# A spectral layer's second exchange: two of eight back steps copied inside SBUF, the others read back from DRAM one back step at a time

## The chip, the cores and the metric

The kernel runs on one core of a Trainium2 chip. The metric is the device time of one execution in microseconds; less is better. In the traces PE is TensorE, DVE is VectorE, ACT is ScalarE, POOL is GpSimd and SP is SyncE, which here issues nearly all DMAs. Times inside an execution count from the start of the profiled span.

## The reference

The input x has 2048 rows (S) of 512 columns (D), in bfloat16. Two layers alternate, twice each:

```python
def _A_ref(x, w_r, w_i):
    X = jnp.fft.rfft2(x.astype(jnp.float32), axes=(-2, -1))
    X = X * (w_r + 1j * w_i)
    return jnp.fft.irfft2(X, s=(S, D), axes=(-2, -1)).astype(jnp.bfloat16)

x = x + _A_ref(_layernorm(x), A_w_r, A_w_i)      # spectral layer
x = x + _B_ref(_layernorm(x), wq, wk, wv, wo)    # attention: 32 heads of 16, one shared key and value head
x = x + _A_ref(_layernorm(x), A_w_r, A_w_i)
x = x + _B_ref(_layernorm(x), wq, wk, wv, wo)
```

The change is in the spectral layer. It filters x in the two-dimensional frequency domain and transforms back.

## The kernel before

Each spectral layer is written as matrix products with tables of sines and cosines, in bfloat16, with sums in PSUM. The 2048 rows are split as 128 by 16, so a transform over the rows takes two products with an exchange of partitions between them. Columns are in two halves (h = 0, 1) of 128 frequencies, real and imaginary part side by side, 256 values in all.

Forward, `forward` (L275) transforms the columns, `first` (L285 by way of `rotate`, L214 to L216) does the first product over the rows, and the result goes to DRAM (D1, L290) and comes back with other partitions (A2, `cross1`, L293). This is the first exchange; it isn't changed.

Then the layer works in eight back steps, j = 0 to 7. Steps 0 to 3 belong to half 0 and steps 4 to 7 to half 1; each covers four blocks b of the 16. `filtered(j)` (f) does the forward product of these blocks, evicts it (ACT, L339) and multiplies by the filter (DVE, L343 and L345). `back(j)` (b) multiplies with the tables H1, H2, H2N, H1N, two blocks to a PSUM bank, evicts the bank into B1 (L375 on ACT; the last bank of step 7 on DVE, L373), and writes these two blocks of B1 to the DRAM buffer D2 (L376, on SP's queue). The tables H are made on POOL by `blocks` (L266), as the product of a small table HC and a mask.

The second exchange is `cross2` (L379): one call reads a quarter of the rows t of D2 into B2, for all 128 partitions. Each half takes four such reads of 256 KB. A read needs all four back steps of its half, since every row of B2 holds something of each. The reads of half 0 are the step x0 in a list of steps written out by hand (`STEPS`, L50):

```python
STEPS = "f0 f1 f2 b0 f3 b1 b2 j f4 b3 x0 f5 f6 b4 f7 b5 j7 b6 b7"
```

After the list, `along(q, 0)` (L401) multiplies B2 of half 0 by the table CS, two rows t at a time, eight times, and ACT and DVE in turn evict into AT (L404, L406). Then the four reads of half 1 are issued, two from SP and two from ACT, then the loads of wq and wo (L1225, L1226, in the first layer). TensorE starts the first four `last(t, 0)` (L414 to L416), which need half 0 only, and goes on with `along(q, 1)` (L401 again) and the rest of `last`. ACT evicts the result into x_sb (L435), and layer norm statistics (L157) and the first projections of attention (L472) follow.

The order on each engine's queue is the order of the program text (`manual_schedule`), and an instruction that waits holds up those behind it in its queue. DMAs issued by one engine complete on semaphores that are used in turn. Attention is planned ahead, when the program is built, and its order doesn't depend on times on the chip. The spectral layer occurs twice, at 0 to 92 us and at about 704 to 784 us of the span.

Of the kernel before, what the change touches and what calls it, by code (L numbers as in the profile page):

```python
# [10 lines left out]
ALU = mybir.AluOpType  # L11
P = 128
BF = mybir.dt.bfloat16
# [4 lines left out]
S, D, H, DH = 2048, 512, 32, 16  # L18
# [28 lines left out]
LASTW = 6  # L47
NEGATE = 7
DIRECT = (0, 2, 4, 6)
STEPS = "f0 f1 f2 b0 f3 b1 b2 j f4 b3 x0 f5 f6 b4 f7 b5 j7 b6 b7"  # L50
NORMED, NORMG = (1,), ((3,), (3,), (3,))
OUTK, LATE_AT = 2, 4
TWICE = ((7,), 8)
# [23 lines left out]
def host_tables():  # L77
    import ml_dtypes
    bf = lambda a: np.ascontiguousarray(np.asarray(a, dtype=np.float32).astype(ml_dtypes.bfloat16))
    tabs = {}  # L80
    p = np.arange(P, dtype=np.float64)
    m = np.arange(P, dtype=np.float64)
    t16 = np.arange(16, dtype=np.float64)

    row = (128 * np.arange(4)[None, :, None] + np.arange(P)[:, None, None]).astype(np.float64)
    ff = (np.arange(256)[None, None, :] + 1).astype(np.float64)

    half = 2 * np.pi * np.arange(256) / 512.0
    cos, sin = np.cos(half), np.sin(half)
    cos[128], sin[0] = 0.0, 0.0  # L90
    cos[129:], sin[129:] = -cos[1:128][::-1], sin[1:128][::-1]
    turn = (row * ff).astype(np.int64) % 512
    c, s = np.concatenate([cos, -cos])[turn], -np.concatenate([sin, -sin])[turn]
    tabs["PH"] = bf(np.concatenate([c[..., :128], s[..., :128], c[..., 128:], s[..., 128:]], axis=2))

    ang = 2 * np.pi * (16 * p[:, None, None] + t16[None, :, None]) * m[None, None, :] / 2048.0
    tabs["C1"], tabs["S1"] = bf(np.cos(ang)), bf(np.sin(ang))

    ti, ai = np.divmod(np.arange(P), 8)
    same = (ai[:, None] == ai[None, :]).astype(np.float64)  # L100
    ang = 2 * np.pi * ti[:, None] * ti[None, :] / 16.0
    tabs["G"] = bf(np.stack([same * np.cos(ang), same * np.sin(ang), -same * np.sin(ang)], axis=1))

    b16 = np.arange(16, dtype=np.float64)
    mm = 16 * ai[:, None, None] + b16[None, :, None]
    ang = 2 * np.pi * (ti[:, None, None] * t16[None, None, :] / 16.0 + t16[None, None, :] * mm / 2048.0)
    tabs["HC"] = bf(np.stack([np.cos(ang), np.sin(ang), -np.sin(ang), -np.cos(ang)], axis=1))
    tabs["mask8"] = bf(ai[:, None] == np.arange(8)[None, :])

    ang = 2 * np.pi * m[:, None] * p[None, :] / 128.0  # L110
    tabs["CS"] = bf(np.stack([np.concatenate([np.cos(ang), np.sin(ang)], axis=1),
                              np.concatenate([-np.sin(ang), np.cos(ang)], axis=1)], axis=1))

    frow = (128 * np.arange(2)[None, :, None] + np.arange(P)[:, None, None] + 1).astype(np.float64)
    dd = np.arange(512)[None, None, :].astype(np.float64)
    ang = 2 * np.pi * frow * dd / 512.0
    cf = np.where(frow == 256, 1.0, 2.0) / (S * D)
    tabs["PSC"] = bf(cf * np.cos(ang))
    tabs["PSS"] = bf(-cf * np.sin(ang))
    tabs["ident"] = bf(np.eye(P, dtype=np.float32))  # L120
    tabs["hmask"] = (np.arange(P)[:, None] // DH % 2 == np.arange(2)[None, :]).astype(np.float32)
    return tabs


class Tables:


    def __init__(self, nc):
        self.nc, self.host, self.dram = nc, host_tables(), {}
# [82 lines left out]
def rotate(nc, ps, c, s, sn, re_im, first, begin=True, end=True):  # L212

    nc.tensor.matmul(ps, lhsT=c, rhs=re_im, start=begin, stop=False, skip_group_check=True)  # L214
    nc.tensor.matmul(ps[:, 0:128], lhsT=s, rhs=re_im[:, 128:256], start=False, stop=False, skip_group_check=True)
    nc.tensor.matmul(ps[:, 128:256], lhsT=sn, rhs=re_im[:, 0:128], start=False, stop=end, skip_group_check=True)  # L216


def spectral_layer(nc, tc, tabs, ht, A_w_r, A_w_i, x_sb, bigp, pre, norm, att, feed, weights):
    C1, S1, S1N, PH, ident = (tabs[n] for n in ("C1", "S1", "S1N", "PH", "ident"))  # L220
    with tc.tile_pool(name="workA", bufs=2) as work, tc.tile_pool(name="tabA", bufs=1) as tabA, \
# [31 lines left out]
            weights(k)  # L253

        D1 = dram.tile([2, 16, P, 256], BF, name="D1")
        D2 = dram.tile([2, P, 16, 256], BF, name="D2")
        turned = len(feed.xT)
        xT = feed.xT[0] if turned else bigp.tile([P, NC, 16, P], BF, name="xT", tag="big")
        Pk, A1, A2 = big("Pk"), big("A1"), big("A2")
# [1 line left out]
        def blocks(q):  # L261

            b = slice(4 * q, 4 * q + 4)
            shape = [P, 4, 16, 8]
            for i, H in enumerate([H1[:, b], H2[:, b], H2N[:, b]] + ([H1N[q]] if q in H1N else [])):
                nc.gpsimd.tensor_tensor(out=H.rearrange("p b (t a) -> p b t a", a=8),  # L266
                                        in0=tabs["HC"][:, i, b].unsqueeze(3).to_broadcast(shape),
                                        in1=tabs["mask8"].unsqueeze(1).unsqueeze(1).to_broadcast(shape), op=ALU.mult)

        def forward(k, h):  # L270

# [26 lines left out]
        for k in range(9 + behind):  # L298
# [6 lines left out]
            at = k - behind  # L305
# [21 lines left out]
        Z, B1, B2 = big("Z"), big("B1"), big("B2")  # L327
        M = big("M").rearrange("p h t c -> p (h t c)").rearrange("p (i j b r f) -> p i j b r f", i=2, j=4, b=4, r=2)

        def filtered(j):  # L330

            h, b4 = j // 4, 4 * (j % 4)
            hf = slice(128 * h, 128 * h + 128)
            X = work.tile([P, 4, 2, 128], BF, name="X", tag="X", bufs=3)
            for b in range(b4, b4 + 4, 2):
                ps = bank()
                for i in range(2):
                    rotate(nc, ps[:, i, :], G[:, 0, :], G[:, 1, :], G[:, 2, :], A2[:, h, b + i, :], i == 0)
                nc.scalar.copy(out=X[:, b - b4:b - b4 + 2, :, :], in_=ps.rearrange("p j (r f) -> p j r f", r=2))  # L339
            m1, m2 = (M[:, i, j % 4] for i in range(2))  # L340
            wrb = wr_sb[:, b4:b4 + 4, hf].unsqueeze(2).to_broadcast([P, 4, 2, 128])
            wib = wi_sb[:, b4:b4 + 4, hf].unsqueeze(2).to_broadcast([P, 4, 2, 128])
            nc.vector.tensor_tensor(out=m1, in0=X, in1=wrb, op=ALU.mult)  # L343
            joined()
            nc.vector.tensor_tensor(out=m2, in0=X, in1=wib, op=ALU.mult)  # L345
            if j in DIRECT:
                unsummed[j] = (m1, m2)
            else:
                products.append((j, m1, m2))
# [3 lines left out]
        def joined():  # L353

            while products:
                j, m1, m2 = products.pop()
                Zv = Z[:, j // 4, 4 * (j % 4):4 * (j % 4) + 4, :].rearrange("p b (r f) -> p b r f", r=2)
                nc.vector.tensor_tensor(out=Zv[:, :, 0, :], in0=m1[:, :, 0, :], in1=m2[:, :, 1, :], op=ALU.subtract)
                nc.vector.tensor_tensor(out=Zv[:, :, 1, :], in0=m1[:, :, 1, :], in1=m2[:, :, 0, :], op=ALU.add)

        def back(j):
            h, b4 = j // 4, 4 * (j % 4)
            for b in range(b4, b4 + 4, 2):
                ps = bank()
                for i in range(2):
                    if j in DIRECT:
                        m1, m2 = (m[:, b + i - b4].rearrange("p r f -> p (r f)") for m in unsummed[j])
                        rotate(nc, ps[:, i, :], H1[:, b + i, :], H2N[:, b + i, :], H2[:, b + i, :], m1, i == 0, True, False)
                        rotate(nc, ps[:, i, :], H2N[:, b + i, :], H1N[j % 4][:, b + i - b4, :], H1[:, b + i, :], m2, False, False)
                    else:  # L370
                        rotate(nc, ps[:, i, :], H1[:, b + i, :], H2N[:, b + i, :], H2[:, b + i, :], Z[:, h, b + i, :], i == 0)
                if j == 7 and b > b4:
                    nc.vector.tensor_copy(out=B1[:, h, b:b + 2, :], in_=ps)  # L373
                else:
                    nc.scalar.copy(out=B1[:, h, b:b + 2, :], in_=ps)  # L375
                nc.sync.dma_start(out=D2[h, :, b:b + 2, :], in_=B1[:, h, b:b + 2, :])  # L376

        def cross2(h, g, eng):
            eng.dma_start(out=B2[:, h, 4 * g:4 * g + 4, :],  # L379
                          in_=D2[h].rearrange("(t a) b c -> t (a b) c", t=16)[4 * g:4 * g + 4].rearrange("t m c -> m t c"))  # L380

        for step in STEPS.split():
            j = int(step[1:] or 0)
            if step[0] == "f":
                filtered(j)
            elif step[0] == "b":
                back(j)
            elif step[0] == "j":
                joined()
            else:  # L390
                for g in range(4):
                    cross2(0, g, nc.sync)

        AT = big("AT").rearrange("p h t c -> p (h t c)").rearrange("p (t h c) -> p t h c", t=16, h=2)

# [21 lines left out]

        for q in range(8):
            along(q, 0, q % 2 == 0)
        for g in range(4):  # L420
            cross2(1, g, (nc.sync, nc.scalar)[g % 2])
        weights(20)
        early = 4
        for t in range(early):
# [2 lines left out]
        for q in range(9):  # L427
# [9 lines left out]
            g, odd = divmod(q - 3, 2)  # L437
# [863 lines left out]
```

## Time and profile before

| | us |
|---|---|
| median of 3 runs | 1403.78 |
| lowest and highest run | 1402.68, 1403.95 |
| profiled execution, its time | 1402.49 |
| its span | 1400.7 |
| TensorE busy | 1348.2 (96%) |
| ScalarE busy | 1331.4 (95%) |
| VectorE busy | 1305.8 (93%) |
| GpSimd busy | 849.4 (61%) |
| DMA D2<-B1 (L376), 128 KB, issue to landing | 3.0 median of 32 |
| DMA B2<-D2 (L379), 256 KB, issue to landing | 3.9 median of 12 on SP, 4.4 median of 4 on ACT |
| DMA A2<-D1 (L293), 256 KB, issue to landing | 3.3 median of 16 |

The profile names a tile without its number, so B is B1 or B2, D is D1 or D2, and A is A1 or A2. "SPq" is SP's queue: an issue of a DMA, not the transfer. In the chain of work that ended last, each line is a start, a length and what ran; a DMA there runs from its issue to its landing. In the timeline a bracket gives the idle time ahead of an instruction and what ended it. In the table by stretches, the last two columns are the mean busy share of the core's 16 DMA engines and the GB/s that they moved.

### The profile page before, as it was taken

What the parts mean: (1) busy time and instruction counts of PE and PEld (TensorE: products, weight loads), DVE (VectorE), ACT (ScalarE), POOL (GpSimd) and SP (SyncE); (2) the same over time, 40 slices, a digit from 0 to 9 for tenths busy, and PEclk for the clock granted to TensorE, in tenths of its full rate; (3) what the DMA queues carried; (4) which work ended last, traced back from release to release, by engine and by line L of the source; (5) the groups of instructions that cost most, each with busy time, mean ns of one, the idle gap of its engine ahead of it and who ended that gap; (6) DMA issues with size and microseconds to landing.
All of it is one profiled execution on the core that took longest, in us unless ns stands there. A gap on an engine that the chain in (4) does not pass through costs nothing.

```text
span 1400.7 us, 35023 instructions
## 1 busy us (share of the span) xinstructions
PE 1348.2 (96%) x14146; PEld 477.7 (34%) x14214; DVE 1305.8 (93%) x2253; ACT 1331.4 (95%) x1542; POOL 849.4 (61%) x507
## 2 busy tenths in 40 slices
PE   7899999999999999999999999999999999999998
PEld 6752232222222222222277422322223222222222
DVE  5689999999999999999966899999999999999997
ACT  6679999999999999999957899999999999999997
POOL 3325666667666667666640367666667667666664
PEclk9999999999999999999999999999999999999999
DMA  8700000000000000002064000000000000000000
GB/s 243 209 17 2 1 2 2 2 2 2 2 1 1 2 2 2 2 1 37 11 166 137 2 2 2 2 1 9 5 6 2 6 9 5 2 6 5 9 2 16
DMA packets 45395, 32.70 MB, mean 23 GB/s; under 512 B 10160, under 2 KB 43184, under 8 KB 44720
## 3 DMA queue, kind: packets, MB, share of 16 engines
q1 hardware_dynamic: 42832, 29.24, 7.4%
q8 instruction: 111, 1.82, 0.5%
q10 hardware_dynamic: 2400, 1.21, 0.3%
q14 instruction: 52, 0.43, 0.1%
HBM read 18.39 MB, written 10.49 MB: 21 GB/s over the span
## 4 chain that ended last, share of the span: by engine, by line
ACT 48%; PE 33%; issue 9%; DVE 6%; DMA 2%; POOL 1%; SPq 0%; DVEq 0%; ACTq 0%; POOLq 0%
ACT e L1099 47%; PE pv L888 13%; PE sc L933 10%; DVE ph L973 3%; PE aux L933 2%; PE ps L214 1%; PE ps L275 1%; DVE ln_stats L157 1%; PE aux L472 1%; DMA B<-D 1%; DVE ph L1005 1%; PE pv L903 1%; PE aux L701 1%; POOL tab_H L266 1%; PE ps L216 1%
## 5 line engine op out<-in xcount | busy, mean ns | idle before, releaser
L1099 ACT ACTIVATE e<-sc 128x1024 bf16<-128x1024 f32 x1328 | 1218.1, 1163 | 2.9 <-PE sc L933 2.9
L997 POOL TENSOR_TENSOR ph<-ph,step 128x1024 int32<-128x1024 int32 x404 | 763.3, 1893 | 412.3 <-DVE ph L1005 291.8
L973 DVE TENSOR_SCALAR ph<-aux 128x512 uint16<-128x512 f32 x1440 | 904.0, 679 | 20.4 <-PE aux L933 15.8
L888 PE MATMUL pv<-ph,vaug 128*32 128x512 bf16 x4320 | 548.8, 386 | 0.6 <-POOL ph L997 0.3
L933 PE MATMUL sc<-QT,Kv 32*128 32x512 bf16 x2656 | 521.9, 380 | 23.2 <-ACT e L1099 15.9
L888 PE MATMUL pv<-e,vaug 128*32 128x512 bf16 x2656 | 484.0, 384 | 0.3 <-ACT e L1099 0.3
L933 PE MATMUL aux<-QT,Kv 32*128 32x512 bf16 x1440 | 456.0, 384 | 1.0 <-DVE ph L973 0.5
L933 PEld LDWEIGHTS <-Kv 32*128 32x128 bf16 x4096 | 183.2, 91 | 525.5 <-issue 517.2
L903 PE MATMUL pv<-wo_sb,zeros 128*32 128x512 bf16 x1200 | 257.9, 383 | 0.0
L888 PEld LDWEIGHTS <-vaug 128*32 128x32 bf16 x6976 | 147.7, 94 | 293.0 <-issue 282.0
L1005 DVE TENSOR_SCALAR ph<-ph 128x2048 uint16<-128x2048 uint16 x316 | 216.6, 685 | 0.5
L163 POOL TENSOR_TENSOR ln_rstd<-ln_veps,mhalf 128x4 f32<-128x4 f32 x16 | 16.5, 1034 | 107.2 <-DVE ln_veps L162 107.1
L157 DVE BATCH_NORM_STATS2 ln_stats<-x_sb 128x6 f32<-128x512 bf16 x64 | 43.5, 679 | 23.3 <-ACT x_sb L435 17.2
L903 PEld LDWEIGHTS <-zeros 128*32 128x32 bf16 x1200 | 60.1, 94 | 1.9 <-issue 0.3
L803 DVE STREAM_TRANSPOSE oT<-pv 128x512 f32<-128x512 f32 x64 | 45.3, 707 | 9.2 <-PE pv L888 9.2
L186 ACT ACTIVATE Pk<-ps,ln_rstd 128x256 bf16<-128x256 f32 x64 | 26.7, 473 | 21.0 <-PE ps L275 16.1
L289 DVE CAST A<-ps 128x512 bf16<-128x512 f32 x28 | 19.2, 689 | 19.8 <-PE ps L216 18.7
L275 PE MATMUL ps<-tab_PH,xT 128*128 128x256 bf16 x256 | 35.6, 288 | 1.7 <-DMA tab_PH<-const_PH 0.8
L472 PE MATMUL aux<-xTa,wq_sb 128*128 128x512 bf16 x90 | 32.6, 385 | 2.8 <-issue 2.4
L825 POOL TENSOR_TENSOR on<-oT,rden 128x512 bf16<-128x512 f32 x30 | 31.7, 1058 | 2.0 <-DVE rden L829 1.8
L701 PE MATMUL aux<-wo_sb,ph 128*128 128x512 bf16 x72 | 26.1, 383 | 3.6 <-issue 2.1
L275 PEld LDWEIGHTS <-xT 128*128 128x128 bf16 x256 | 25.4, 103 | 6.0 <-issue 1.5
(117 smaller groups left out, 715.2 us busy)
## 6 DMA issues: line engine op xcount, KB each, us to landing
D<-A SPq DMA_DIRECT2D x32, 128.0 KB, 2.7
A<-D SPq DMA_DIRECT2D x16, 256.0 KB, 3.3
D<-B SPq DMA_DIRECT2D x32, 128.0 KB, 3.0
B<-D SPq DMA_DIRECT2D x12, 256.0 KB, 3.9
wr_sb<-in_A_w_r_dram SPq DMA_DIRECT2D x2, 1024.0 KB, 7.0
wi_sb<-in_A_w_i_dram SPq DMA_DIRECT2D x2, 1024.0 KB, 8.9
out_dram<-x_sb SPq DMA_DIRECT2D x15, 128.0 KB, 1.7
x_sb<-in_A_x_dram SPq DMA_DIRECT2D x3, 512.0 KB, 8.2
```

Source lines behind the costliest of these rows:

```text
L157: nc.vector.bn_stats(st, src)
L275: nc.tensor.matmul(ps[:, j, :], lhsT=xT[:, cc, 2 * k + j, :], rhs=PH[:, cc, 256 * h:256 * h + 256], start=(cc == 0), stop=(cc == NC - 1), ...
L472: self.nc.tensor.matmul(ps, lhsT=w(c), rhs=self.xTq[:, c, qc * 512:(qc + 1) * 512], start=(c == 0), stop=(c == NC - 1), skip_group_check=True)
L701: nc.tensor.matmul(ps, lhsT=OTs[qb][:, g4, kk * P:(kk + 1) * P], rhs=wo_sb[:, g4, :], start=first, stop=last, skip_group_check=True)
L803: end = clock.now(clock.FLIP, lambda: nc.vector.transpose(out=oT[:, par].rearrange("p b c -> p (b c)"), in_=pv), clock.last + clock.MM_END)
L888: nc.tensor.matmul(pv_tiles[gi][32 * i:32 * i + 32, :], lhsT=vaug[:, kc, j, :], rhs=es, start=((gi, i) not in started), stop=(left[gi, i] ...
L903: nc.tensor.matmul(pv_tiles[gi][32 * i:32 * i + 32, :], lhsT=att.zeros, rhs=wo_sb[:, 0, :], start=False, stop=False, skip_group_check=True)
L933: nc.tensor.matmul(out, lhsT=Kv[r, par, kc * P:(kc + 1) * P], rhs=QT[r, g, qb * 512:(qb + 1) * 512], start=True, stop=True, skip_group_che ...
L973: end = clock.now(clock.Z, lambda: nc.vector.tensor_scalar(out=z.bitcast(U16), in0=ps, scalar1=SCALE * LOG2E * 128.0, scalar2=127.0 * 128. ...
L997: nc.gpsimd.tensor_tensor(out=copy.bitcast(I32), in0=z.bitcast(I32), in1=step.to_broadcast([P, w // 2]), op=ALU.add)
L1005: nc.vector.tensor_scalar(out=one.bitcast(U16), in0=z.bitcast(U16), scalar1=float(PHASE[1]), scalar2=None, op0=ALU.add)
L1099: nc.scalar.activation(out=e[:, 0:ng * 512], in_=sc[:, 0:ng, :].rearrange("p a b -> p (a b)"), func=ACT.Exp, scale=SCALE)
```

## The change

B2 is laid out by another rule. Its partitions are ordered by back step (32 to a step), so that one back step fills 32 partitions with all sixteen rows t. D2 is laid out by half, back step, block and partition. For back steps 0 to 5, `back` writes two blocks to D2 as before, in pieces of 512 bytes, and `cross2(h, g)` reads one back step (256 KB) in runs of 8 KB, 32 of them. For steps 6 and 7, `back` copies each block (64 KB, 128 pieces of 512 bytes) straight from B1 into eight partitions of B2, each four partitions from the next; no write to D2 and no read is left for them. The four reads of half 0 stay together (x0 to x3); the two reads left of half 1 (x4 and x5) stand behind b6 and b7 in the list, all on SP's queue. To match, the tables H have their columns in the order (a t) instead of (t a), and the rows of the table CS are permuted.

```diff
-STEPS = "f0 f1 f2 b0 f3 b1 b2 j f4 b3 x0 f5 f6 b4 f7 b5 j7 b6 b7"
+STEPS = "f0 f1 f2 b0 f3 b1 b2 j f4 b3 x0 x1 x2 x3 f5 f6 b4 f7 b5 j7 b6 x4 b7 x5"
...
-                              np.concatenate([-np.sin(ang), np.cos(ang)], axis=1)], axis=1))
+                              np.concatenate([-np.sin(ang), np.cos(ang)], axis=1)], axis=1)[16 * (np.arange(P) // 4 % 8) + 4 * (np.arange(P) // 32) + np.arange(P) % 4])
...
-        D2 = dram.tile([2, P, 16, 256], BF, name="D2")
+        D2 = dram.tile([2, 4, 4, P, 256], BF, name="D2")
...
-            shape = [P, 4, 16, 8]
+            shape = [P, 4, 8, 16]
...
-                nc.gpsimd.tensor_tensor(out=H.rearrange("p b (t a) -> p b t a", a=8),
-                                        in0=tabs["HC"][:, i, b].unsqueeze(3).to_broadcast(shape),
-                                        in1=tabs["mask8"].unsqueeze(1).unsqueeze(1).to_broadcast(shape), op=ALU.mult)
+                nc.gpsimd.tensor_tensor(out=H.rearrange("p b (a t) -> p b a t", a=8),
+                                        in0=tabs["HC"][:, i, b].unsqueeze(2).to_broadcast(shape),
+                                        in1=tabs["mask8"].unsqueeze(1).unsqueeze(3).to_broadcast(shape), op=ALU.mult)
...
-                nc.sync.dma_start(out=D2[h, :, b:b + 2, :], in_=B1[:, h, b:b + 2, :])
-
-        def cross2(h, g, eng):
-            eng.dma_start(out=B2[:, h, 4 * g:4 * g + 4, :],
-                          in_=D2[h].rearrange("(t a) b c -> t (a b) c", t=16)[4 * g:4 * g + 4].rearrange("t m c -> m t c"))
+                if j >= 6:
+                    for bb in (b, b + 1):
+                        at = 32 * (j % 4) + bb - b4
+                        nc.sync.dma_start(out=B2[at:at + 29:4, h, :, :], in_=B1[:, h, bb, :])
+                else:
+                    nc.sync.dma_start(out=D2[h, j % 4, b - b4:b - b4 + 2].rearrange("b p c -> p b c"), in_=B1[:, h, b:b + 2, :])
+
+        def cross2(h, g):
+            nc.sync.dma_start(out=B2[32 * g:32 * g + 32, h, :, :],
+                              in_=D2[h, g].rearrange("b (a t) c -> a b (t c)", t=16))
...
-                for g in range(4):
-                    cross2(0, g, nc.sync)
+                cross2(j // 4, j % 4)
...
-        for g in range(4):
-            cross2(1, g, (nc.sync, nc.scalar)[g % 2])
```

## The prediction, made before the changed kernel ran

> **What bounds the kernel now.** I read the page first (busy shares and the chain that ended last), then the chain in order of time around the second exchange, then TensorE's timeline at the one place where it waits, then SP's timeline and the DMA stretches for prices.
>
> ```profile
> span 1400.7 us, 35023 instructions
> ACT 48%; PE 33%; issue 9%; DVE 6%; DMA 2%; POOL 1%; SPq 0%; DVEq 0%; ACTq 0%; POOLq 0%
> ```
>
> Attention (ACT's exponentials and TensorE) carries the span. DMA is on the chain for 2%, about 28 us, and two short pieces of that are the second exchange. The chain in order of time, first spectral layer:
>
> ```profile
> 58.98 0.11 PE ps L214
> 59.14 0.07 PE ps L216
> 59.24 0.59 ACT B L375
> 59.83 0.28 SPq L376
> 60.20 0.41 SPq L376
> 60.70 2.93 DMA D<-B
> 63.76 3.35 DMA B<-D
> 67.16 0.62 PE ps L401 x4
> 67.80 0.59 ACT AT L404
> ```
>
> Back step 7 is evicted, written to DRAM (2.93 us), read back (3.35 us), and only then can L401 begin half 1. In the second layer the same three pieces stand at 752.65 (2.99 us), 755.76 (3.32 us) and 759.12. But TensorE is busy for most of those 6.3 us with half 0 and with the first four `last` steps:
>
> ```profile
> 65.13 0.38 PE L415 MATMUL ps<-tab_PSC,AT 128*128 128x512 bf16 x1
> 65.34 0.38 PE L416 MATMUL ps<-tab_PSS,AT 128*128 128x512 bf16 x1
> 67.16 0.61 PE L401 MATMUL ps<-tab_CS,B 128*128 128x256 bf16 x4 [1.43 <-DMA B<-D]
> ```
>
> The wait that is left is 1.43 us here and 1.46 us in the second layer. **The whole exchange can give back at most 2.89 us**, 0.206% of 1402.49 us, however fast it becomes: below that TensorE's own queue ends at 65.72. (About 0.2%, 2.8 us, is what a measurement of this kernel tells from no change.)
>
> **What leaves the path.** The DRAM write of back steps 6 and 7 and the four reads of half 1 go; b6 and b7 now write eight 64 KB copies inside SBUF, and reads x4 and x5 fetch what b4 and b5 wrote long before. So 2.93 + 3.35 us in series become one transfer. ACT loses two DMA issues (1.00 us at 63.77); it is idle until 67.80 there, so that is worth nothing. TensorE, VectorE and ScalarE run the same instructions otherwise. L401 of half 1 now waits for all of B2, on eight semaphores; before, it waited for one quarter at a time, and the first quarter set the start, so what counts now is the last landing.
>
> **SP's queue.** Rows of SP's timeline:
>
> ```profile
> 46.96 5.82 SPq L376 DMA_DIRECT2D D<-B  x8
> 54.55 2.50 SPq L379 DMA_DIRECT2D B<-D  x4
> 57.09 4.01 SPq L376 DMA_DIRECT2D D<-B  x8
> 63.76 0.92 SPq L379 DMA_DIRECT2D B<-D  x2
> ```
>
> An issue takes 0.4 us and the next starts 0.47 us after it. b3's writes leave SP at 52.8; the four old reads then waited for their landing until 54.55. Now x0, x1, x2 need only older writes and go at 52.85, 53.3, 53.8; x3 waits until 54.55. The tail grows from 4 writes and 2 reads to 8 copies and 2 reads. ACT hands over b6's first pair at 58.25 (57.70 + 0.55), so by issue time alone SP would end: copies 58.25, 58.72, 59.20, 59.67, x4 60.14, copies 60.6 to 62.0, x5 62.5. In the built program eight DMA semaphores are used in turn, and an issue waits for the DMA that had its semaphore before: b6's fourth copy for x3, x4 for b4's two writes, b7's copies for b5's writes and b6's first copy, x5 for b6's second. Behind x5 stand only the loads of wq and wo (landing 6.1 and 7.0 us); L472 needs wq at 81.1, so 10 us cover them.
>
> **The DMA engines.** This decides. The new reads are 8 KB runs dealt as 8 outer rows, the new copies go to 8 partitions. No transfer of this trace has fewer than 32 outer rows, so their price is bounded: all 16 engines serve them, or 8 do. I take 8, since eight rows are not dealt evenly over more. Prices per engine: with 512 B rows the 16 engines move 341 GB/s (21.3 each); the isolated A<-D read, whose runs are 8 KB too, reaches 395 GB/s (24.7 each) in its best half us and 215 (13.4 each) over its whole length.
>
> ```profile
> 66.00:67.00 1.00, 0.00 (x0) 0.00 (x0) 0.00 (x0) 0.00 (x0) 0.00 (x0) 1.00 1.14 341
> ...
> 736.25:736.75 0.50, 0.50 (x10) 0.48 (x9) 0.50 (x2) 0.39 (x1) 0.00 (x0) 1.00 1.01 395
> 736.00:737.25 1.25, 1.19 (x17) 1.13 (x16) 1.25 (x4) 0.93 (x3) 0.00 (x0) 1.00 0.59 215
> ```
>
> The work of each of the eight engines, from x0 to x5: six reads of 32.8 KB at 24.7 GB/s, 1.33 us each, 7.98; four writes of b4 and b5 (8.2 KB each at 21.3, 0.385 us), 1.54; eight copies of 8.2 KB, 3.08 (no SBUF to SBUF copy is in the trace; the 512 B write is the nearest row; from nothing to the 0.6 us that 13.4 GB/s would give). Together 12.6 us. Data begins 1.1 us after an issue (issue 63.76, DMA share 0.07 from 64 to 65 and 0.77 from 65 to 66), and the shortest A<-D lands 2.9 us after its issue, of which 0.66 is data at 395 GB/s, so 1.14 us follow. Sum: 52.85 + 1.1 + 12.6 + 1.14 = **67.7**, against 67.11 before (63.76 + 3.35). By this SP's waits bind nowhere, because the engines' backlog is longer. The stall on DRAM is replaced by a stall on half the DMA engines, 0.58 us longer per layer.
>
> On the way x3 lands at 52.85 + 1.1 + 5.3 + 1.14 = 60.4, while TensorE wants half 0 at 59.48: a new wait of 0.9 us, hidden, because half 0 then ends at 66.6 and the join is later still.
>
> The Trainium skill (DMA: Bandwidth & Descriptors, section "Why a DMA increments its semaphore by 16 and not by 1") speaks against this change: a DMA runs on the largest number of engines up to 16 that divides the outermost count of both sides. By that rule both new forms run on 8; no run here shows it yet. The same page (section Specifications) gives about 27 GiB/s per engine; with that the 12.6 would be 10.2 us, an estimate, and the join 65.3, which is rival B's time.
>
> **Mask tables on POOL.** L266 now writes (a t) instead of (t a): the broadcast operand changes sides, 14 instructions per layer. In the second layer they are on the chain (704.95 to 719.18) ahead of ln_rstd, for which ACT waits 2.0 us. They take 1037 ns undisturbed. L825 on POOL has the new form (second operand broadcast over a run of 16) at the same 512 elements: 1057 ns. Bounds: 14 x 0.02 = +0.3 us, and a gain of at most that 2.0 us; I take 0, since the rate follows the element count (1024 elements take 1893 ns at L997).
>
> **Sum.** 2 x 0.58 = +1.2 us. The profiled execution took 1402.49 us (span 1400.7 and 1.8 around it), 1.3 below the median of the runs, 1403.78. So 1405.0 as a median.
>
> **Rivals.**
> A, the forecast: half the engines, backlog about as late as the old round trip. At 21.3 GB/s for the 8 KB runs a read takes 1.54 us and the layer loses 1.8; at 30.8 (the best quarter us, 492 GB/s over 16) it gains 1.0. Within 0.2%: 1402 to 1406.6.
> B, the stall goes: all 16 engines serve the new transfers, or the eight are faster than the rows. Then x5, issued at 62.5, lands 2.9 to 3.3 us later, at 65.4 to 65.8, TensorE does not wait, and 1.35 to 1.44 us per layer are saved: 1400.9 to 1401.1. For it: 395 GB/s in bursts, and the earlier x0 to x2. Against: the eight outer rows.
> C, slower: the long runs drag. If eight engines sustain under 22.3 GB/s on 8 KB runs, six reads per layer end over 1.4 us late and the loss passes 0.2%. At the mean of 395 and 215 GB/s, 19.1 each, a read takes 1.72 us: 10.3 + 4.6 = 14.9, join 70.0, 2.9 us per layer, **1409.6**. For it: the A<-D read needs over 1 us for 2 runs per engine. Against: there 16 engines read at once, here 8. At 13.4 GB/s it would be 1418; I hold that end unlikely, since four runs queue on each engine instead of two.
> D, the copies or POOL's tables cost something that no row shows; either sign.
>
> **How the numbers follow.** A 0.45, B 0.20, C 0.27, D 0.08. Faster by over 0.2% needs nearly the whole 2.89 us: half of B and a little of D, 0.12. Slower by over 0.2%: C and some of D, 0.30. The rest, 0.58, within 0.2%. The range takes in B at 1400.8 and C's nearer half, up to 1409.0; left out are C's far half and a little below B.
>
> **What would show it.** Right: L401 of half 1 starts near 67.7 and 759.7 and waits for a DMA into B2; x0 to x5 land late, 4 us or more after issue; DMA moves about 200 GB/s between 54 and 66 instead of 340; half 0 waits for x3. B: L401 follows `last` without a gap and x reads land in about 3 us. C: half 0 waits 2 us or more, half 1 begins near 70. Wrong altogether: L266 away from 1.04 us, or a difference outside 44 to 68 and 736 to 760 us.

## The result, and the profile after

Four runs of the changed kernel had a median of 1411.47 us (1410.97 to 1412.92), those of the kernel before 1403.87 us: ratio 1.0052, 95% interval 1.0038 to 1.0065. The change costs some 7.6 us, more than the top of the predicted range (1409.0). The two profiled executions are further apart (1412.92 and 1402.49 us), since one is the slowest of its four and the other faster than any of its four; so below the trace tells where the loss sits and the medians how large it is.

The page's span and its shares of the chain, after:

```profile
span 1411.1 us, 35028 instructions
ACT 49%; PE 32%; issue 9%; DVE 6%; DMA 2%; POOL 1%; SPq 1%; DVEq 0%; ACTq 0%; POOLq 0%
```

Nothing large has moved; SP's queue now has 1% of the chain. The chain in order of time, first spectral layer (start, length, what ran):

```profile
56.76 5.48 DMA D<-B
62.30 0.69 SPq L384
63.03 0.63 SPq L379
63.70 0.61 SPq L379
64.31 0.06 issue
64.42 0.61 SPq L379
65.07 0.61 SPq L379
65.72 5.20 DMA B<-D
70.97 1.26 PE ps L405 x8
72.26 0.61 PE ps L419
```

The two DMAs in series are still there, and longer: 5.48 and 5.20 us where 2.93 and 3.35 stood. They are other DMAs than was meant. The first is a write of back step 4, which x4 waits for; the second is the read x5; between them SP spends 3.4 us on issuing x4 and the four copies of b7. Half 1 begins at 70.97 us, 3.81 later than before. In the second layer a write of 6.21 us leads to x4 at 760.20, x5 is issued at 763.62 and lands at 768.08, and half 1 begins at 768.28.

TensorE's timeline, after (in the bracket the idle time ahead, and what ended it):

```profile
61.70 3.65 PE L405 MATMUL ps<-tab_CS,B 128*128 128x256 bf16 x32 [1.92 <-DMA B<-D]
67.56 0.38 PE L420 MATMUL ps<-tab_PSS,AT 128*128 128x512 bf16 x1
70.97 1.26 PE L405 MATMUL ps<-tab_CS,B 128*128 128x256 bf16 x8 [3.03 <-DMA B<-D]
72.66 0.63 PE L420 MATMUL ps<-tab_PSS,AT 128*128 128x512 bf16 x1
```

Two waits stand where there was one of 1.43 us: 1.92 us for x3 and 3.03 us for x5. The last line shows a third loss: the same matmul that took 0.38 us at 67.56 takes 0.63 at 72.66. The table by stretches (PEclk is the third column from the right) says why:

```profile
70.00:71.00 1.00, 0.03 (x1) 0.03 (x2) 0.00 (x0) 0.00 (x0) 0.00 (x0) 1.00 0.85 271
71.00:72.00 1.00, 1.00 (x8) 0.68 (x8) 0.00 (x0) 0.38 (x1) 0.00 (x0) 0.83 0.90 319
72.00:73.00 1.00, 0.97 (x4) 0.28 (x3) 0.00 (x0) 0.79 (x2) 0.00 (x0) 0.50 0.30 105
75.00:76.00 1.00, 1.00 (x6) 0.48 (x5) 0.68 (x2) 0.96 (x2) 0.00 (x0) 0.96 0.00 0
```

Behind the idle stretch the granted clock is 0.50 until about 75 us. Attention's first exponential comes at 98.40 us, 5.18 late: 3.81 from the join, the other 1.4 from this clock. In the second layer it comes at 795.43 instead of 785.19, 10.24 late; 5.5 of these had come from the first layer, so the second adds some 4.7. Together that is nearly all of the 10.4 us between the two spans.

SP's timeline, after:

```profile
53.12 3.11 SPq L384 DMA_DIRECT2D B<-D  x4
56.28 2.01 SPq L381 DMA_DIRECT2D D<-B  x4
58.45 3.63 SPq L379 DMA_DIRECT2D B<-B  x4
62.30 0.69 SPq L384 DMA_DIRECT2D B<-D  x1
63.03 2.64 SPq L379 DMA_DIRECT2D B<-B  x4
65.72 0.68 SPq L384 DMA_DIRECT2D B<-D  x1
```

x5 leaves SP at 65.72 us; the prediction had 62.5. The nine issues from b6's first copy up to x5 should have taken 4.2 us and took 7.3. The nine alone took 5.8 us, where 0.4 each had been expected, so some 2 of the 3 us more are longer issues; 0.9 are waits (by the list of waits, 0.7 for the read x3 ahead of a copy and 0.2 for the write ahead of x4).

**Landings.** The trace also has the semaphore events of each DMA. A read of 8 outer rows shows one early event and then eight, a transfer of 32 or more rows sixteen. The first write of b4 landed in two parts: eight events at 58.01 to 58.12, the other eight at 61.52 to 61.86, behind x0 to x3. The table gives the mean spacing of the landings of x0 to x3 (256 KB each; a DMA counted at the median of its engines' events, the early one left out), and the median time of one 8 KB piece of these reads in the trace's record of DMA packets, in us, with the runs told of below:

| reads | spacing, layers 1 and 2 | one 8 KB piece, layers 1 and 2 |
|---|---|---|
| before: 128 partitions, pieces of 512 B, 16 engines | 1.06, 0.90 | - |
| after: 32 neighbouring partitions, 8 rows | 1.41, 1.56 | 0.31, 0.31 |
| the same, no copies (e2) | 1.87, 1.33 | 0.32, 0.31 |
| 32 neighbouring partitions, 32 rows (e1) | 1.18, 1.16 | 0.62, 0.57 |
| the same, no copies (e3) | 1.27, 1.15 | 0.62, 0.60 |
| every fourth partition, 8 rows (e7) | 1.35, 1.74 | 0.31, 0.45 |
| every fourth partition, 32 rows (e5) | 0.86, 1.04 | 0.31, 0.31 |
| the same, with copies (e6) | 0.96, 0.92 | 0.31, 0.31 |

A read is 32 pieces: four to an engine with eight engines, two with sixteen. Four at 0.31 are 1.24 us, and the shortest gap between reads of the change is 1.23 in the first layer and 1.32 in the second; two at 0.31 are 0.62, and the shortest gap in e5 is 0.64. Into 32 neighbouring partitions the pieces of sixteen engines take about 0.6 us each; two of them are 1.2 again, so sixteen engines gain little there.

### The profile page after: what moved, and what is told of

Its sections match the earlier page's. It is cut to its first block, busy times and chain, and to the rows that moved or that the text cites. A ratio compares the mean times of both kernels' runs of the same rounds, so it can differ in the third digit from the quotient of the medians.

```text
span 1411.1 us, 35028 instructions
## 1 busy us (share of the span) xinstructions
PE 1350.2 (96%) x14146; PEld 477.9 (34%) x14214; DVE 1307.0 (93%) x2253; ACT 1331.5 (94%) x1542; POOL 850.2 (60%) x507
## 4 chain that ended last, share of the span: by engine, by line
ACT 49%; PE 32%; issue 9%; DVE 6%; DMA 2%; POOL 1%; SPq 1%; DVEq 0%; ACTq 0%; POOLq 0%
ACT e L1101 48%; PE pv L890 12%; PE sc L935 10%; DVE ph L975 3%; PE aux L935 2%; PE ps L275 1%; PE ps L214 1%; DMA D<-B 1%; DVE ph L1007 1%; PE aux L474 1%; PE ps L419 1%; DVE ln_stats L157 1%; PE ps L420 1%; PE pv L905 1%; PE aux L703 1%
## 5 line engine op out<-in xcount | busy, mean ns | idle before, releaser
L408 ACT CAST AT<-ps 128x512 bf16<-128x512 f32 x24 | 14.2, 590 | 19.7 <-PE ps L405 16.7
```

## The experiments

The theory: eight engines carry the reads, the writes of b4 and b5 queue behind them there, and so SP's queue stands still ahead of x4. The rivals: the copies are what costs; 8 KB runs are slow in themselves; the clock makes up most of it.

**Reads of 32 rows (e1).** The partitions of a back step go block by block, so that a read has 32 outer rows of 8 KB.

```diff
-[16 * (np.arange(P) // 4 % 8) + 4 * (np.arange(P) // 32) + np.arange(P) % 4])
+[16 * (np.arange(P) % 8) + 4 * (np.arange(P) // 32) + np.arange(P) // 8 % 4])
-                        at = 32 * (j % 4) + bb - b4
-                        nc.sync.dma_start(out=B2[at:at + 29:4, h, :, :], in_=B1[:, h, bb, :])
+                        at = 32 * (j % 4) + 8 * (bb - b4)
+                        nc.sync.dma_start(out=B2[at:at + 8, h, :, :], in_=B1[:, h, bb, :])
-                              in_=D2[h, g].rearrange("b (a t) c -> a b (t c)", t=16))
+                              in_=D2[h, g].rearrange("b (a t) c -> (b a) (t c)", t=16))
```

> The new layout with the partitions of a back step ordered block by block, so that each read has 32 outer rows of the same 8 KB runs; the copies stay, into 8 partitions side by side. Theory (eight outer rows halve the DMA engines and lengthen the issue): a read lands in about 3 us instead of 4.0 to 5.9, its issue takes 0.4 us instead of 0.68, half 0 does not wait for x3, the join comes near 67.4 us, time 1403 to 1406. Rival 1 (8 KB runs are slow on any engines): reads still land in 4 us or more, time 1409 to 1412. Rival 2 (the copies are the cost, by their issue of 0.61 us and their eight engines): reads get fast, but half 1 still waits 2 us or more, time 1407 to 1411.

Measured 1410.96 us against 1404.63, ratio 1.0045 (1.003 to 1.006). Half 0 waited 1.21 us instead of 1.92 and the issue of a read fell from 0.68 to 0.38 us, but half 1 began where it had:

```profile
70.80 1.05 PE L405 MATMUL ps<-tab_CS,B 128*128 128x256 bf16 x8 [3.89 <-DMA B<-D]
```

So the theory's branch failed, and the time is the one that rival 2, the copies, gave. A read still took 1.16 to 1.18 us, well over what twice the engines would give. And e1 is no clean test of the reads: its edit also sends each copy into 8 neighbouring partitions, and b7's four copies then landed 0.86 to 1.15 us apart, against 0.36 to 0.42 in the change. The read x5 shares the engines with them in e1, so how much of that is the copies' new place isn't shown.

**No copies (e2, e3).** All eight back steps go through DRAM, in e2 with the change's rows, in e3 with those of e1.

```diff
-... b6 x4 b7 x5"
+... b6 b7 x4 x5 x6 x7"
-                if j >= 6:
+                if j >= 8:
```

> The changed kernel without the copies inside SBUF: back steps 6 and 7 go through DRAM too, and x4 to x7 stand behind b7. The reads keep their 8 outer rows. Theory (eight outer rows): eight reads of 1.4 us and eight writes share the low engines, the join comes at 69 to 71 us, time 1409 to 1414. Rival 2 (the copies are the cost): clearly faster than the changed kernel, below 1407.

> No copies inside SBUF, and reads of 32 outer rows: only the reading by back step in 8 KB runs is left of the change. Theory (eight outer rows): the last read is issued near 63 and lands near 66, half 1 hardly waits, the kernel is as fast as the one before or up to 2.5 us faster, 1401 to 1404. Rival 1 (8 KB runs are slow): 1409 or more, like the run with 8 rows.

Measured: e2 1413.95 us, ratio 1.0071 (1.0048 to 1.0094); e3 1405.61 us, ratio 1.0008 (0.9996 to 1.002). TensorE's timelines, e2:

```profile
64.00 5.32 PE L405 MATMUL ps<-tab_CS,B 128*128 128x256 bf16 x32 [2.71 <-DMA B<-D]
73.83 1.03 PE L405 MATMUL ps<-tab_CS,B 128*128 128x256 bf16 x8 [1.93 <-DMA B<-D]
```

and e3:

```profile
60.65 3.65 PE L405 MATMUL ps<-tab_CS,B 128*128 128x256 bf16 x32 [1.37 <-DMA D<-B]
68.83 1.03 PE L405 MATMUL ps<-tab_CS,B 128*128 128x256 bf16 x8 [1.93 <-DMA B<-D]
```

Without copies, the step from 8 rows to 32 is worth 8 us, and it alone brings the time back to that of the kernel before, within the interval. With copies it gave nothing that could be told, but there the copies had become slower too. The copies in e1's form cost 5 us (e1 against e3); what they cost in the change's own form is answered by e6 below. In e2 the 32 matmuls of half 0 take 5.32 us instead of 3.65: there the clock fell already ahead of half 0.

**A warm TensorE (e4).** The change, with 13 matmuls of no use between the first four `last` steps and half 1; their result is thrown away.

```diff
+        warm = psum.tile([P, 512], F32, name="ps", tag="pa")
+        for _ in range(13):
+            nc.tensor.matmul(warm, lhsT=ident, rhs=PSC[:, 0, :], start=True, stop=True, skip_group_check=True)
```

> The changed kernel with 13 idle matmuls on TensorE (2.8 us, into an unused bank) in the wait ahead of half 1; the wait itself stays. If the clock of 0.5 that the profile shows for about 3 us after that wait costs what it seems, the clock stays at 1.0 there and each layer gains 1.2 to 1.5 us: 1408 to 1409.5. If the clock is only a symptom and DMA sets the pace there too, the time stays at 1411.

Measured 1410.44 us, ratio 1.0043 (1.0028 to 1.0059). The clock stayed at 1.00 through the place where the change had 0.50:

```profile
71.00:72.00 1.00, 1.00 (x8) 0.53 (x6) 0.00 (x0) 0.00 (x0) 0.00 (x0) 1.00 1.02 338
72.00:73.00 1.00, 0.78 (x8) 0.45 (x5) 0.00 (x0) 0.62 (x2) 0.00 (x0) 1.00 0.88 306
```

```profile
71.74 1.04 PE L405 MATMUL ps<-tab_CS,B 128*128 128x256 bf16 x8
75.19 0.60 PE L405 MATMUL ps<-tab_CS,B 128*128 128x256 bf16 x4
```

From the start of half 1 to its third group of matmuls 3.45 us passed (71.74 to 75.19), as before the change (3.46) and against 4.83 in the change. So by the trace the clock costs some 1.4 us in this layer. But half 1 is as late as ever, and the time missed the 1408 to 1409.5 that were expected; that the median falls at all isn't shown, since the interval overlaps that of the change. The clock isn't most of the loss.

**Spread partitions (e5, e6, e7).** A new question from e1 and e3: why does a read take 1.15 us on 16 engines, when the kernel before took 0.90 to 1.06 with pieces sixteen times smaller? Its reads went to all 128 partitions, these to 32 neighbours. So back step g was given the partitions 4i + g. In e5 (all through DRAM, 32 rows):

```diff
-[16 * (np.arange(P) // 4 % 8) + 4 * (np.arange(P) // 32) + np.arange(P) % 4])
+[16 * (np.arange(P) // 4 % 8) + 4 * (np.arange(P) % 4) + np.arange(P) // 32])
-            nc.sync.dma_start(out=B2[32 * g:32 * g + 32, h, :, :],
+            nc.sync.dma_start(out=B2[g:g + 125:4, h, :, :],
```

e6 is that with the change's copies (`at = 32 * (bb - b4) + j % 4`, again every fourth partition); e7 is e5 with 8 outer rows.

> Like the run whose reads had 32 outer rows and which had no copies (1405.61 us, half 1 starting at 68.83), but each step's 256 KB lands in every fourth of the 128 partitions instead of in 32 neighbouring ones; 8 KB runs, 16 engines and SP's order stay. If the ports of 32 neighbouring partitions set the 1.1 to 1.2 us of each read, a read costs about the 0.77 us that the reads of the kernel before took into 128 partitions, four reads end 1.6 us sooner, half 1 starts near 67.2 us and the time is 1401.5 to 1403.5 us. If 8 KB runs are slow in themselves, nothing moves: 68.8 us and 1405 to 1406 us.

> The change with reads of 32 outer rows and the spread partitions: reads on 16 engines into every fourth partition, the copies of one block into 8 partitions at stride 4 as in the change. If the ports are the limit, x0 to x3 need about 0.8 us each, b4's writes land sooner, copies are 0.41 us apart again and half 1 starts between 67.5 and 69 us: 1403 to 1407 us. If copies and SP's waits are the limit whatever the reads cost, half 1 stays near 70.8 us: about 1411 us.

> No copies and 8 outer rows, so 8 engines and SP's issues of 0.65 us, as in the run of 1413.95 us (half 1 at 73.83 us), but into spread partitions. If the number of engines sets a read's time, it stays at 1412 to 1415 us. If only the ports did, a read falls to about 0.8 us and SP's issue of 0.65 us is next: half 1 near 69 us, 1405 to 1408 us.

Measured, against 1404.12 us: e5 1404.12, ratio 1.0000 (0.9991 to 1.0009); e6 1406.08, ratio 1.0018 (1.0009 to 1.0027); e7 1416.52, ratio 1.0093 (1.0079 to 1.0107). TensorE at half 1, e5:

```profile
67.46 1.03 PE L405 MATMUL ps<-tab_CS,B 128*128 128x256 bf16 x8 [1.70 <-DMA B<-D]
```

and e6:

```profile
67.31 1.05 PE L405 MATMUL ps<-tab_CS,B 128*128 128x256 bf16 x8 [1.49 <-DMA B<-D]
```

With 16 engines, spreading takes a read from 1.15 to 1.27 us to 0.86 to 1.04, and one 8 KB piece from about 0.6 us to 0.31. So 8 KB runs aren't slow in themselves; what limited them was where they landed. (The same reads in e9, e11 and e12 were 0.85 to 1.08 us apart, in e10 1.32 and 1.04; in the layer with 1.32 a single issue on SP took 1.61 us.) The Trainium skill (SBUF — State Buffer, section "Door 1: The DMA port swizzle (why `[64,N]` ≈ `[32,N]`)") says that 32 neighbouring partitions reach 8 of 16 ports, at about 27 GB/s each; that would be 1.2 us for 256 KB, an estimate, and the row is 1.15 to 1.27. For the whole kernel, with the copies in, e1 to e6 goes from 1.0045 to 1.0018 and the intervals are apart, though this step spreads the copies as well as the reads; without copies, e3 to e5, they overlap. e5's expected gain over the kernel before didn't come: its half 1 starts at 67.46, near the 67.2 that were expected, but the kernel before had 67.16. e7 is a miss on its cheap branch, and a little above the dear one: with 8 rows, spreading does not help (1.35 and 1.74 us). The number of engines is a limit of its own: without copies its mending was enough (e3), with copies the time comes near that of the kernel before only with both mended (e6). And e6 against e5: the copies still cost some 2 us, and gain nothing.

**SP's order (e8, e9).** e8 is the change with x4 behind b7's copies (`b6 b7 x4 x5`); e9 is e6 with x4 and x5 ahead of all copies (`x4 x5 b6 b7`).

> The change with x4 issued behind b7's copies, not ahead of them, and nothing else. If SP's wait for b4's writes ahead of x4 holds back b7's copies and x5 is late for that, x5 is issued later still or at the same time (65.7 us), since SP's issues are the same in number; half 1 starts within 0.5 us of 70.97 us and the time is 1410 to 1412 us. If the wait itself costs (as the rivals have it), half 1 starts 1 us or more sooner: under 1409.5 us.

> The run with 16 engines, spread partitions and copies (1406.08 us, half 1 at 67.31), with x4 and x5 issued on SP ahead of all copies. There x5 was issued at 64.36 though the writes that it reads had landed by 60.4, so what held it was SP's row of copies. If SP's order is what is left of the loss, x5 is issued at 60.5 and is no longer last; the eight copies follow at 0.62 us each and the last lands near 66.5: half 1 at 66.6 to 66.8, 1404 to 1406 us. If the transfers themselves are the limit, half 1 stays at 67.3 or later.

Measured: e8 1411.08 us, ratio 1.0050 (1.0037 to 1.0063), as expected: nothing moved by more than the run's scatter. SP's rows of e8:

```profile
59.68 6.23 SPq L379 DMA_DIRECT2D B<-B  x8
65.95 1.40 SPq L384 DMA_DIRECT2D B<-D  x2
```

Eight copies and two reads need SP until 67 us in either order, so x5 goes out late in both. e9 1410.6 us against 1405.01, ratio 1.0033 (1.0022 to 1.0045): I expected a gain over e6 and got none, rather a loss (the intervals just overlap; half 1 starts 8.96 and 10.01 us behind half 0 in e9's layers, 7.73 and 8.45 in e6's). SP's rows of e9, and TensorE's:

```profile
56.61 2.86 SPq L381 DMA_DIRECT2D D<-B  x4
61.53 1.16 SPq L384 DMA_DIRECT2D B<-D  x2
62.78 5.47 SPq L379 DMA_DIRECT2D B<-B  x8
```

```profile
69.96 1.89 PE L405 MATMUL ps<-tab_CS,B 128*128 128x256 bf16 x8 [2.72 <-DMA B<-B]
```

SP stood still from 59.47 to 61.53 for the writes of b4, with eight copies behind it whose first data ACT had ready at about 60.4. x5 is no longer last; the copies are. That is the plainest sight of SP's wait binding: its place in the queue only decides who pays.

**Off SP's queue, and fewer copies (e10, e11, e12).** e10 is e9 with x4 and x5 issued by POOL (`(nc.sync, nc.gpsimd)[h].dma_start`), e11 is e6 with only b7 copied (`if j >= 7`, `b6 x4 x5 x6 b7`), e12 is e11 with x4 to x6 on POOL.

> As the run before, with x4 and x5 on POOL's queue, which is idle then, so that their wait holds nothing and SP has only writes and copies. If SP's order was all that was left, the copies of b7 are issued by 63.8 and land by 65, x5 has landed by 64, and TensorE goes from half 0 into half 1 without a wait (65.8 us): 1.5 us less in each layer than the kernel before, 1401 to 1402.5 us against its 1404. If a DMA of POOL costs microseconds of its own (no row of this case shows one), x5 stays last and the time is 1404 us or more.

> 16 engines and spread partitions, only the last step b7 copied inside SBUF, x4 to x6 read on SP ahead of the four copies. Four issues of 0.62 us fewer on SP: if SP's row is the limit, x6 waits for b6's writes (landed near 62) and is issued at 62.3, the copies of b7 at 62.4 to 64.9, the last landing near 66: half 1 at 65.9 to 66.5, 1401.5 to 1404 us. If copies are slow whoever stands ahead of them, half 1 is at 67 or later and the time 1404 to 1406 us.

> The run in which only b7 is copied (1404.97 us against 1405.01 of the kernel before), with x4 to x6 on POOL's queue. There SP waited 0.7 and 0.5 us for writes ahead of x4 to x6, and issued b7's copies at 754.35 to 757.04 although their data was ready near 752. If SP's row is what is left, the copies are issued by 755, the last lands by 757.5 and half 1 starts with at most 0.5 us of wait: 1402 to 1403.5 us against 1404.5 to 1405 of the kernel before. If the engines are, which x4 to x6 then share with the copies (as when x4 and x5 were on POOL, where the last copy landed at 761.3, 3.6 us after its issue), half 1 waits 1 us or more as before and the time is within 0.1% of the kernel before.

Measured: e10 1405.02 us, ratio 0.9996 (0.9986 to 1.0006); e11 1404.97, ratio 0.9996 (0.9987 to 1.0005); e12 1405.78, ratio 1.0009 (0.9999 to 1.0019). No version beats the kernel before. e10 is level with it, and 5.6 us under e9, with intervals that are apart: what x4 and x5 held back on SP's queue was the whole of e9's loss. e11, with half as many copies, is under e6 (0.9987 to 1.0005 against 1.0009 to 1.0027). But the gain that e10 to e12 were to bring isn't there. e10 missed the 1401 to 1402.5 us, and not for the reason that was named (the copies are last, not x5); e11 and e12 came out on the dearer branch of what was expected. TensorE in the second layers, e10:

```profile
761.56 1.03 PE L405 MATMUL ps<-tab_CS,B 128*128 128x256 bf16 x8 [2.64 <-DMA B<-B]
```

e11:

```profile
759.11 1.05 PE L405 MATMUL ps<-tab_CS,B 128*128 128x256 bf16 x8 [1.76 <-DMA B<-B]
```

Counted from the start of half 0, half 1 came after 7.32 us (e10) and 7.30 (e11) in the first layer, where the kernel before had 7.68: a gain of some 0.4 us. In the second layer it came after 8.89 and 8.00, where the kernel before had 7.70. The chain of e10 there has the last copy, and that of e12 a write and a read:

```profile
756.81 4.51 DMA B<-B
```

```profile
752.15 3.88 DMA D<-B
756.54 3.73 DMA B<-D
```

The semaphore events show that these long transfers waited for one engine. Of the eight engines of e10's last copy, seven had landed by 759.82 us and the eighth at 761.32. Of the sixteen of e12's write, which x6 waits for, fifteen had landed by 754.45, before the first data of x4 (754.86), and the last at 756.02. So x4 and x5 were not what held it up. In both stretches the trace has a 16 KB packet of the kind "instruction", a kind of its own beside the packets of the kernel's DMAs: in e12 it starts at 753.28 us, between issue and landing of the write, and takes 1.56 us; in e10 it starts at 753.98, among the copies, and one engine stays behind the others from there to the last copy.

```profile
q8 instruction: 1, 0.02, 4.9%
```

This is a line of e12's DMA queues from 753 to 755 us: one packet, 0.02 MB, and its share of the 16 engines' time. That the packet sits on just the engine that is late is inferred from the times; the trace doesn't name the engine. At the join of the first layers this is absent: there e10's last copy leaves SP at 66.08 and all eight engines land it by 67.91, and what is left is a wait of 1.07 us in e10, 1.06 in e11 and 1.36 in e12, against 1.43 before. What remains open is how much a kernel with fewer bytes in flight just then, or with these packets at another time, would gain; no run varied either.

## Why the prediction was wrong

The direction of the likeliest case (slightly slower) was right, its size was not: 1405.0 predicted, 1411.47 measured. Rival C's 1409.6 and its join at 70.0 came nearer, but by luck: its condition, eight engines that sustain under 22.3 GB/s, did not hold, since one 8 KB piece took 0.31 us, 26 GB/s. By its own steps:

- **"By this SP's waits bind nowhere, because the engines' backlog is longer."** This step failed. The engines' work and SP's queue were taken as two chains of which the longer counts, 67.7 against some 65.8 (x5 issued at 62.5 and landing 3.3 us later). Each waits for the other. The writes of b4 use all sixteen engines and stood behind x0 to x3 on eight of them (landing in two parts, 58.1 and 61.9 us). SP waits for x3 and for these writes before x4, at 62.30, and the copies of b7 and x5 stand behind x4. So x5 left SP at 65.72, 3.2 us later than by SP's own count. Even x0, the first of the reads, took 4.0 us from issue to landing in both layers, not 3.3; 65.72 and 4.0 make 69.7, past the predicted join already. The other 1.2 us x5 lost on the engines, behind b7's copies and with the load of wq issued right after it; in the second layer, where no such load follows, it lost 0.5. Which of the two costs more isn't shown.
- **The backlog of 12.6 us.** Its prices were right: 24 pieces of 8 KB at 0.31 us and 192 of 512 B at 0.027 us, the medians of the packets, are 12.6 us for one engine again. What failed is that it runs without a break. With the prediction's own 1.1 us ahead and 1.14 behind, the stretch from x0 to x5 took 15.6 us in the first layer and 15.5 in the second; DMA moved 89 GB/s from 54 to 56 us and 134 from 64 to 66. Where the 3 us went is known in part: x4, late on SP, landed 1.8 us behind the last copy of b6 and x5 2.85 behind that of b7, where 1.33 were reckoned; in the second layer x2 came 2.5 us behind x1, and why is open. That SP's queue can bind is shown by e9 and e10 (a wait ahead of eight copies, and the same wait on POOL: 5.6 us apart), though with the reads of 32 rows; in the change's own form no run took the wait away.
- **The issue of 0.47 us** was mis-sized: 0.68 for an 8-row read, 0.61 for a copy, plus some 0.04. That is about 2 us of the 3.2, more than the 0.9 us of waits. e1 shows that the rows matter for it (0.38 us).
- **The read of 1.33 us** was near, on the low side: 1.41 and 1.56 us in the change; the copy of 0.385 too (0.36 to 0.42 apart). That the new forms run on eight engines was right; the Trainium skill's rule that I cited against the change (DMA: Bandwidth & Descriptors, section "Why a DMA increments its semaphore by 16 and not by 1") holds here: eight late events and one early one for 8 rows. What I had not weighed was the side where the data lands, which alone keeps a read at 1.15 us or more on all sixteen.
- **"About 200 GB/s between 54 and 66 instead of 340"** could tell nothing: from 54 to 66 us the kernel before moved 195 GB/s on average, the changed one 179.
- **The hidden wait of half 0.** It came as said, larger (1.92 and 2.48 us instead of 0.9), and it was hidden behind the join as said.
- **TensorE runs "the same instructions otherwise".** True, but not at the same clock. Behind the wait for x5 (3.03 and 2.53 us) 1.1 to 1.4 us more per layer were lost at 0.50 of the clock; no term stood for it.
- **POOL's tables at no cost** were right: L266 took a median of 1.04 us in both kernels.
- **At most 2.89 us to gain**: no run contradicts it, and no version came near. The stall on DRAM was cheap, since TensorE hid all but 1.43 us of it, and every way that was tried to avoid it used the engines or the queue that the rest needed.

## What to carry to other kernels

When a transfer is moved onto fewer DMA engines, look for the transfers that still use all of them: they finish with the slowest, and whatever waits for them on an issuing queue holds back that queue's later work. Before counting a DMA's time by its bytes, look at both ends of its pattern: how many outer rows it has, and which partitions it lands in. A DMA is done when its slowest engine is, so look at the last of its semaphore events before you put a wait down to other traffic. And where the wait to be removed is 1.4 us, first ask what the new way keeps busy in the last 8 us before it.

## What the runs showed that was not expected

- SP's issue time depends on the pattern, not on the bytes: 256 KB reads took a median of 0.68 us with 8 rows into neighbouring partitions, 0.58 with 8 rows spread, 0.38 with 32 rows into neighbours, 0.54 with 32 spread. Why is open.
- TensorE's clock fell after some waits and not after others: after 3.03 us in the change, and after 1.76 us in the second layer of e11 (0.50 from 760.8 to 764.2 us), but not after 3.00 us ahead of half 0 in e4, nor after 2.64 us in e10. The Trainium skill (TensorE: Matmul & The Clock Gate, section "Part 1: The HAM clock gate (the "warmup" mystery)") says that the clock halves after an idle window of about 3.4 us, and that the windows run freely. That the same wait does or does not count agrees with windows that run freely; that 1.76 us can be enough does not agree with a wholly idle window. No run here varied it.
- One engine in sixteen is often late, and with it the whole DMA. Of the transfers of this exchange in all fourteen traces, 29 had their last semaphore event more than 1 us behind the one before. In 22 of them a 16 KB "instruction" packet (median 0.96 to 1.15 us) started between issue and landing, and six of the other seven are transfers of e10, issued one behind the other after such a packet; of the remaining 628 transfers, 129 had one start in that time. Every trace has 111 of these packets, that of the kernel before included. That they are the cause is argued from these times, not tested.
